# Two-stage packed attention and a mixer in one kernel: which engine copies the keys, when the first attention and w1's pieces are worked on, and in which iterations w2's pieces are made

## The chip, the core and the metric

The kernel runs on one core of a Trainium2 chip. A core has TensorE (PE in the profile, its weight loads PEld), VectorE (DVE), ScalarE (ACT), GpSimd (POOL) and SyncE (SP), which here issues all transfers. The metric is the device time of one execution in microseconds (us). Smaller is better.

## The reference

There are 8 batches of 8 heads, 576 tokens and 64 elements per head. A short sequence p of 32 tokens per head first attends to all keys; the 576 queries then attend to its 32 results. The output of all heads is x (576 by 512), and a mixer with float64 weights follows:

```python
p_packed = sm_attn(p, k, v)              # sm_attn: softmax(q k^T / 8) v
out = sm_attn(q, p_packed, p_packed)     # x = out, heads side by side: 8 x 576 x 512
h = x^T @ U @ V                          # over tokens, rank 32
u = x + h^T
ch = relu(u @ w_ch1) @ w_ch2             # 512 -> 2048 -> 512
return u + ch
```

w_ch1 (w1 below) and w_ch2 (w2) arrive as float64, and the kernel makes float32 of their bits itself.

## The kernel before, in words

**Two parts.** The *front* does the first attention stage for all batches (p against the keys) and makes float32 of w1. The *loop* does the mixer's two matrix products batch by batch, with the second attention stage of a later batch spread between them.

**The front** goes through 16 units, a batch's half of four heads each (`UN`, index i or u). For a unit it transposes the keys on TensorE (`a_turn`, which calls `turn` for h = 0, 1, 2), multiplies them with p (`a_scores`, line 244), takes the maximum on VectorE (line 448, tile mx) and the exponential on ScalarE (line 450), turns the result back (`a_turn_back`, lines 250, 252 and 459), multiplies with the values (`a_pack`, line 478) and turns the heads (`a_heads`, line 488). In `turn`, h = 0 and h = 1 each leave one PSUM bank that two copies of 128x256 empty into SBUF: one on ScalarE (line 231) and, while `split_copies` is True, one on VectorE (line 229). Queries (tile xT) go through the same `turn`.

Beside this the front makes w1's 16 pieces of 128x512 (`some_w1`): ScalarE takes the absolute value (line 143) and VectorE does four operations (lines 78 to 81) into w1t; the load four pieces ahead is issued there as well. `turns[i]` says how many pieces unit i gets. From unit 4 on each unit also takes three of the 24 steps of the second attention stage of batch 0 (`first = attention(0, res)`): query loads, turns, scores, softmax (with two GpSimd operations of 128x576, lines 283 and 294), `tokens` (lines 312, 313), `mix1` and `mix2` (line 333 and, on GpSimd, line 335, which writes al). al and ah are what the loop's first product reads. Steps and `a_p`, `a_heads` and `fold` share the two banks of the pool psT (t_ps). `fold(0, 0)` (lines 372, 378, 379) makes the first part of the folded w1 in unit 13. In the front the framework's planner arranges the instructions on each engine (the context is opened with `schedule_with_timeline_sim=True`), so their order is near the written one but not the same.

**The loop** starts behind `tc.manual_schedule()`: from there each engine works in the written order. For each batch b and each kt of 16, `gemm1(kt)` fills the banks h_ps (lines 86 to 88), ScalarE makes hh by a relu (line 614), VectorE hl (line 617); each half of h_ps has one bank only, so `gemm1(kt+1)` waits until hl(kt) has been made. `gemm2(kt-1)` then adds hh and hl times w2 into four banks o. At kt = 2, 6, 10 and 14 a `fold` follows, and steps of the attention of batch b + 1 (b + 2 in the later batches) are taken before, within and after `gemm2`.

**w2** is made during batch 0, a piece of 128 rows per iteration: `load_w2` (line 151, SP), `convert_w2` (line 77 on ScalarE, lines 78 to 81 on VectorE) and `split_w2` (line 158 on ScalarE, line 159 on VectorE), which leaves the high and the low part that `gemm2` reads. The pool for the bits has two buffers, that for the converted values four. At iteration kt the kernel splits piece kt + 1, loads kt + 3 and converts kt + 2. The place is after the fold and before the iteration's last step:

```python
if w2x:
    split_w2(*w2x)
    w2x = None
    if kt + 3 < NK:
        load_w2(kt + 3)
    if kt + 2 < NK:
        w2x = convert_w2(kt + 2)
```

The steps of batch 1's attention fall into batch 0's iterations as follows: softmax1(0) after w2 in kt = 4, softmax3(0) within gemm2 of kt = 6, softmax4(0) and the second scores in kt = 7, softmax1(1) at the head of kt = 8, softmax3(1) at the end of kt = 9, softmax4(1) in kt = 10, tokens from the end of kt = 11.

Of the kernel before, what the change touches and what calls it, by code (L numbers as in the profile page):

```python
# [19 lines left out]
def packed_attention_mixer_kernel(  # L20
# [37 lines left out]
    NK = DF // P  # L58
# [12 lines left out]
    def float32_of(x, t, raw, out=None, tested=False):  # L71


        low, high = raw[:, :, 0], raw[:, :, 1]
        out = x if out is None else out.bitcast(I32)
        if not tested:
            nc.scalar.activation(t, high.bitcast(F32), AF.Abs)
        nc.vector.tensor_single_scalar(t, t, LEAST, op=ALU.max)  # L78
        nc.vector.tensor_scalar(x, t.bitcast(I32), 3, 0x3FFFFFF8, op0=ALU.logical_shift_left, op1=ALU.bitwise_and)
        nc.vector.scalar_tensor_tensor(x, high, -0x40000000, x, op0=ALU.bitwise_and, op1=ALU.bitwise_or)  # L80
        nc.vector.scalar_tensor_tensor(out, low, 29, x, op0=ALU.logical_shift_right, op1=ALU.bitwise_or)
        return out.bitcast(F32)
# [12 lines left out]
    def bank():  # L95
        return psT.tile([P, 512], F32, name="t_ps", tag="t")
# [25 lines left out]
    def w2_parts(kt):  # L122
        return tuple(t[:, kt % 4] for t in w2t[kt // 4])

    def conv_tile(dtype):
        return pipe.tile([P, DM], dtype, name="os", bufs=4)

    def bits_tile():
        return pipe.tile([P, 512, 2], I32, name="bits", bufs=2)
# [19 lines left out]
    def load_w2(kt):  # L149
        b = bits["w2", kt] = bits_tile()  # L150
        nc.sync.dma_start(out=b.rearrange("p x t -> p (x t)"), in_=w2[kt * P:(kt + 1) * P, :])

    def convert_w2(kt):
        return kt, float32_of(conv_tile(I32), conv_tile(F32), bits.pop(("w2", kt)))

    def split_w2(kt, x):
        hi, lo = w2_parts(kt)
        nc.scalar.copy(hi, x)
        (nc.gpsimd if kt == 0 else nc.vector).tensor_tensor(lo, x, hi.bitcast(F32), op=ALU.subtract)
# [52 lines left out]
            out=x.rearrange("p (h y) -> p h y", h=2),  # L212
            in_=src[b, 4 * g:4 * g + 4].rearrange("(h z) (i c) d -> (z i) h (c d)", z=2, c=NT))

    split_copies = True

    def turn(t, x, h, bank):

        x = x.rearrange("p (h y) -> p h y", h=2)
        t_ps = bank()  # L220
        if h < 2:
            for j in range(4):
                o = P * (2 * (j % 2) + j // 2)
                nc.tensor.transpose(t_ps[:, o:o + P], x[:, h, P * j:P * j + P], ident)  # L224
            src = t_ps.rearrange("p (k a z i) -> p a z k i", k=2, a=2, z=2)
            for a in range(2):
                dst = t[:, 2 * h:2 * h + 2, :4 * I].rearrange("p z (k i a) -> p a z k i", k=2, a=2)[:, a]
                if a and split_copies:
                    nc.vector.tensor_copy(dst, src[:, a])
                else:  # L230
                    nc.scalar.copy(dst, src[:, a])  # L231
        else:
            for h in range(2):
                nc.tensor.transpose(t_ps[:64, P * h:P * h + P], x[:, h, SM:], ident)
            nc.scalar.copy(t[:64, :, LAST], t_ps[:64, :2 * P].rearrange("p (h i) -> p h i", h=4))
# [156 lines left out]
    ua = {}  # L392
    pn, pT, pps, sums = {}, {}, {}, {}

    def bank_a(tag):
        return lambda: psA.tile([P, 512], F32, name=f"{tag}_ps", tag=tag)
# [20 lines left out]
    def a_p(b):  # L417
        t_ps = bank()
        pT[b] = sA.tile([P, 2, P], F32, name="pT")
        pd = sA.tile([P, 2, 2, D], F32, name="pd", bufs=1)  # L420
        nc.gpsimd.tensor_copy(pd, pn[b].unsqueeze(2).to_broadcast([P, 2, 2, D]))
        for i in range(2):
            nc.tensor.transpose(t_ps[:, P * i:P * i + P], pd[:, i].rearrange("p z d -> p (z d)"), ident)
        nc.scalar.activation(pT[b][:, 0], t_ps[:, :P], AF.Copy, scale=scale)
        dst, src = (a.rearrange("p (y z n) -> p z y n", y=2, z=2) for a in (pT[b][:, 1], t_ps[:, P:2 * P]))
        for z in range(2):
            nc.scalar.activation(dst[:, z], src[:, 1 - z], AF.Copy, scale=scale)

    def a_turn(u):
        b, g = UN[u]  # L430
        if g == 0:
            a_p(b)
        ua[u]["t"] = sA.tile([P, 4, 5 * I], F32, name="kT")
        for h in range(3):
            turn(ua[u]["t"], ua[u]["x"], h, bank_a("k"))

    def a_scores(u):
        b, g = UN[u]
        s_ps = psA.tile([P, 1024], F32, name="s_ps", tag="s", bufs=1)
        scores(pT[b], ua[u]["t"], g, (s_ps[:, 512 - 5 * I:512], s_ps[:, 512:512 + 4 * I]))  # L440
        ua[u]["s"] = s_ps[:, 512 - 5 * I:512 + 4 * I]
# [10 lines left out]
    def a_turn_back(u, bank):  # L452
        b, g = UN[u]
        e1 = ua[u]["e"]
        eT = ua[u]["eT"] = sT.tile([P, 5, P], F32, name="eT")
        t_ps = bank()
        for kk in range(4):
            turn_back(t_ps, e1, kk, P * kk)
        nc.scalar.copy(eT[:, :4].rearrange("p k x -> p (k x)"), t_ps)
        t_ps = bank()  # L460
        turn_back(t_ps, e1, 4, 0)
        nc.scalar.copy(eT[:64, 4], t_ps[:64, :P])
        if g == 1 or b == B - 1:
            s = sums[b] if b < B - 1 else sums[b][:, g:g + 1]
            nc.gpsimd.tensor_scalar_add(s, s, 1e-9)
            nc.vector.reciprocal(s, s)
# [43 lines left out]
            load_w1(n + 4)  # L510


    turns = [0, 0, 1, 1, 1, 1, 2, 1, 1, 1, 2, 1, 1, 1, 1, 1]
    n_w1 = 0
    for i in range(NU):
        if i > 0:
            a_turn_back(i - 1, bank_a("m"))
        a_scores(i)
        if i + 1 < NU:
            a_load_v(i + 1)  # L520
            a_turn(i + 1)
        if i + 2 < NU:
            a_load(i + 2)
        a_softmax(i)
        if i < 2:
            load_w1(2 + i)
        for _ in range(turns[i]):
            some_w1(n_w1)
            n_w1 += 1
        if i > 1:  # L530
            a_pack(i - 2, bank_a("m"))
        if i > 2:
            a_heads(i - 3)
        if i >= 4:
            for _ in range(3):
                if first:
                    first.pop(0)()
        if i == 2:
            uv = load_uv()
        if i == 3:  # L540
            prepare_uv(*uv)
        if i == 13:
            fold(0, 0)
        if i == 14:
            load_w2(0)
            load_w2(1)
            steps = attention(1, res)
            steps.pop(0)()
            split_w2(*convert_w2(0))
            load_w2(2)  # L550
# [5 lines left out]
        lambda: (a_heads(NU - 1), tctx.close()),  # L556
    ]
    actx.close()
    split_copies = False


    ctx.enter_context(tc.manual_schedule())
# [118 lines left out]
            nc.sync.dma_start(out=out[b - 1 + i].rearrange("(i c) m -> c i m", c=NT)[8], in_=os_[I * i:I * i + I])  # L681

    w2x = convert_w2(1)

    for n in (20, 19, 18, 15, 15, 14, 13, 12, 12, 11, 5, 0, 0, 0, 0):
        steps.insert(n, lambda: None)
    last, parts = None, []
    for b in range(B):
        cur = Batch(b)
        oj = None  # L690
        ahead = attention(b + 2, res) if b + 2 < B else []
        for kt in range(NK):
            cur.gemm1(kt)
            if oj and kt == 1:
                store_joint(b - 1, oj)
            if steps and (b < 2 or kt % 4 != 2) and (b, kt) != (1, 0):
                steps.pop(0)()
            if (b, kt) == (0, 5):
                w2_tiles(ctx.enter_context(tc.tile_pool(name="sC", bufs=1, side="right", reuse_waits="tile")), 2)
            if kt > 0:  # L700
                cur.gemm2(kt - 1, (rest or steps).pop(0) if b == 0 and (rest or steps) else None)
            elif last:
                last.gemm2(NK - 1)
                last.store()
                if last.b % 2 == 1:
                    oj = joint(last.b, parts)
            if kt % 4 == 2 and (b, kt) != (B - 1, NK - 2):
                n = b * NPC + kt // 4 + 1
                fold(n // NPC, n % NPC)
            if w2x:  # L710
                split_w2(*w2x)
                w2x = None
                if kt + 3 < NK:
                    load_w2(kt + 3)
                if kt + 2 < NK:
                    w2x = convert_w2(kt + 2)
            if steps and kt % 4 != 2 and (b, kt) != (1, 0):
                steps.pop(0)()
            if kt == 1:
                cur.blocks()  # L720
            if kt == 3:
                cur.add_u()
            if ahead and kt == (13 if b else NK - 1):
                ahead.pop(0)()
            if kt == NK - 1 and b % 2 == 1:
                parts = [joint_parts(b, 0), joint_parts(b, 1)]
        assert not steps
        steps = ahead
        last = cur
# [35 lines left out]
```

## Time and profile before

| what | value |
|---|---|
| time, median of 3 runs (lowest to highest) | 846.15 us (845.97 to 846.75) |
| the profiled execution: its own time, its span | 845.35 us, 843.6 us |
| busy: PE, DVE, ACT, POOL | 813.0, 381.5, 328.0, 89.2 us |
| share of the span | 96%, 45%, 39%, 11% |
| read from HBM, written | 46.83 MB, 10.35 MB |

The span goes from the first to the last instruction; the execution's own time has the start and the end around it. Busy shares are means over the whole span, and the front and the loop have different limits, so the rows further down are by stretch. The busy time of PE is modelled at its ends. A wait names what released the waiting instruction last. [...]

### The profile page before, as it was taken

The page shows a single profiled execution, that of the slowest core. Times are in us where ns is not written, and L with a number is a line of the kernel's source. Part 1 is how long each engine was busy: PE and PEld are TensorE (multiplying, and loading weights), DVE is VectorE, ACT ScalarE, POOL GpSimd, SP SyncE. Part 2 cuts the span into 40 slices and gives each one's busy share as a digit, 9 for nine tenths or more (in the row PEclk, how much of TensorE's full clock was granted, in tenths as well). Part 3 has the DMA queues.
Part 4 walks back from the last instruction along what each step waited for, and adds up shares of the span by engine and source line. Part 5 has one row for each costly group of instructions (what it writes and reads, how often), then busy time and mean ns, then how long its engine had stood idle before and what let it go on. Part 6 is the DMA issues. An engine that isn't in the chain of part 4 may idle for free.

```text
span 843.6 us, 14585 instructions
## 1 busy us (share of the span) xinstructions
PE 813.0 (96%) x5800; PEld 653.9 (78%) x5800; DVE 381.5 (45%) x902; ACT 328.0 (39%) x1017; POOL 89.2 (11%) x131
## 2 busy tenths in 40 slices
PE   6888899999999999999999999999999999999997
PEld 4546478778878887888888888888788887888786
DVE  4899676984343333434333234333434234342231
ACT  4667764445233332334233332343234232332231
POOL 1322311100111001010011001010101011100000
PEclk9999999999999999999999999999999999999999
DMA  9999732331001100021001100110001100010001
GB/s 301 347 340 341 237 101 88 101 113 51 1 1 63 51 13 1 1 63 51 1 1 63 50 14 1 44 59 13 1 16 61 51 1 1 1 51 1 1 1 63
DMA packets 36245, 58.13 MB, mean 69 GB/s; under 512 B 9040, under 2 KB 19280, under 8 KB 36176
## 3 DMA queue, kind: packets, MB, share of 16 engines
q1 hardware_dynamic: 36176, 57.19, 20.6%
q8 instruction: 46, 0.75, 0.4%
q14 instruction: 23, 0.19, 0.1%
HBM read 46.83 MB, written 10.35 MB: 68 GB/s over the span
## 4 chain that ended last, share of the span: by engine, by line
PE 86%; DVE 7%; DMA 3%; ACT 2%; issue 1%; SPq 0%; ACTq 0%; DVEq 0%
PE o L86 17%; PE o L88 17%; PE o L87 16%; PE h_ps L86 9%; PE h_ps L88 8%; PE h_ps L87 8%; PE t_ps L372 4%; PE t_ps L224 1%; DMA bits<-in_moe_w_ch_dram 1%; PE t_ps L244 1%; DVE os L80 1%; PE t_ps L320 1%; DVE os L78 1%; DMA x<-in_moe_U_dram 1%; PE t_ps L250 1%
## 5 line engine op out<-in xcount | busy, mean ns | idle before, releaser
L86 PE MATMUL o<-w2h,hh 128*128 128x512 f32 x512 | 206.8, 404 | 0.0
L88 PE MATMUL o<-w2h,hl 128*128 128x512 f32 x512 | 202.5, 396 | 0.0
L87 PE MATMUL o<-w2l,hh 128*128 128x512 f32 x512 | 202.1, 395 | 0.0
L617 DVE SCALAR_TENSOR_TENSOR hl<-h_ps,hh 128x256 fp32r<-128x256 f32 x256 | 104.1, 422 | 201.0 <-ACT hj L616 188.8
L614 ACT ACTIVATE hh<-h_ps 128x256 fp32r<-128x256 f32 x256 | 98.7, 387 | 182.4 <-PE h_ps L88 181.8
L86 PE MATMUL h_ps<-ah,wth 128*128 128x320 f32 (+1 forms) x512 | 157.6, 308 | 2.1 <-DVE hl L617 2.0
L87 PE MATMUL h_ps<-al,wth 128*128 128x320 f32 (+1 forms) x512 | 151.6, 296 | 0.0
L88 PE MATMUL h_ps<-ah,wtl 128*128 128x320 f32 (+1 forms) x512 | 151.4, 296 | 0.0
L86 PEld LDWEIGHTS h_ps<-ah,wth 128*128 128x128 f32 x512 | 96.8, 189 | 34.8 <-issue 27.7
L88 PEld LDWEIGHTS o<-w2h,hl 128*128 128x128 f32 x512 | 96.5, 188 | 22.9
L86 PEld LDWEIGHTS o<-w2h,hh 128*128 128x128 f32 x512 | 96.8, 189 | 21.4 <-issue 4.6
L87 PEld LDWEIGHTS o<-w2l,hh 128*128 128x128 f32 x512 | 96.8, 189 | 16.8
L87 PEld LDWEIGHTS h_ps<-al,wth 128*128 128x128 f32 x512 | 96.9, 189 | 1.8
L88 PEld LDWEIGHTS h_ps<-ah,wtl 128*128 128x128 f32 x512 | 97.0, 189 | 0.0
L379 DVE TENSOR_TENSOR wtl<-t_ps,wth 128x256 fp32r<-128x256 f32 x128 | 48.5, 419 | 96.9 <-ACT wth L378 93.5
L378 ACT CAST wth<-t_ps 128x256 fp32r<-128x256 f32 x128 | 43.3, 374 | 109.2 <-PE t_ps L372 101.4
L335 POOL TENSOR_TENSOR al<-aT,ah 128x320 fp32r<-128x320 f32 (+1 forms) x32 | 25.7, 807 | 207.3 <-ACT ah L334 207.3
L283 POOL TENSOR_TENSOR e<-e,m 128x576 f32<-128x576 f32 x16 | 19.4, 1212 | 251.9 <-DVE m L282 251.9
L231 ACT COPY xT<-t_ps 128x256 f32<-128x256 f32 x60 | 20.3, 393 | 39.2 <-PE t_ps L224 38.5
L372 PE MATMUL t_ps<-w1t,ppT 64*32 64x512 f32 x512 | 35.0, 601 | 0.0
L334 ACT CAST ah<-aT 128x320 fp32r<-128x320 f32 (+1 forms) x32 | 13.7, 433 | 44.1 <-DVE aT L333 44.0
L294 POOL TENSOR_TENSOR e<-e,s 128x576 f32<-128x576 f32 x16 | 18.7, 1166 | 110.3 <-DVE s L293 110.2
(134 smaller groups left out, 964.7 us busy)
## 6 DMA issues: line engine op xcount, KB each, us to landing
bits<-in_moe_w_ch_dram SPq DMA_DIRECT2D x32, 512.0 KB, 5.2
kx<-in_k_dram SPq DMA_DIRECT2D x16, 576.0 KB, 7.1
x<-in_q_dram SPq DMA_DIRECT2D x16, 576.0 KB, 4.9
vt<-in_v_dram SPq DMA_DIRECT2D x32, 256.0 KB, 6.9
out_dram<-bits SPq DMA_DIRECT2D x32, 256.0 KB, 2.4
vt<-in_v_dram SPq DMA_DIRECT2D x16, 64.0 KB, 6.7
out_dram<-os SPq DMA_DIRECT2D x8, 128.0 KB, 2.3
ppTd<-ppTa SPq DMA_DIRECT2D x7, 128.0 KB, 3.7
```

What stands on the lines that cost most here:

```text
L86: nc.tensor.matmul(ps, lhsT=lh, rhs=rh, start=start, stop=False)
L87: nc.tensor.matmul(ps, lhsT=lh, rhs=rl, start=False, stop=False)
L88: nc.tensor.matmul(ps, lhsT=ll, rhs=rh, start=False, stop=stop)
L231: nc.scalar.copy(dst, src[:, a])
L283: nc.gpsimd.tensor_tensor(e, e, m.unsqueeze(2).to_broadcast([P, S // 32, 32]), op=ALU.subtract)
L294: nc.gpsimd.tensor_tensor(e, e, s.unsqueeze(2).to_broadcast([P, S // 32, 32]), op=ALU.mult)
L335: nc.gpsimd.tensor_tensor(al[:, g, ns], aT[:, ns], ah[:, g, ns].bitcast(F32), op=ALU.subtract)
L372: nc.tensor.matmul(f_ps[g][xs], lhsT=ppT[b][zs, g, xs], rhs=w1t[h // 2][zs, QW * c:QW * c + QW], start=True, stop=True)
L378: nc.scalar.copy(hi[:, g], f_ps[g][:, cs])
L379: nc.vector.tensor_tensor(lo[:, g], f_ps[g][:, cs], hi[:, g].bitcast(F32), op=ALU.subtract)
L614: nc.scalar.activation(hh[:, ms], src, AF.Relu)
L617: nc.vector.scalar_tensor_tensor(hl[:, ms], src, 0.0, hh[:, ms].bitcast(F32), op0=ALU.max, op1=ALU.subtract)
```

## The change

Three things change. First, `split_copies` goes; `turn` has an argument `split` that is False unless it is given, and `a_turn` gives True for h = 1 only. So in the front the second copy of h = 0, and the second copies of batch 0's queries, go to ScalarE. In the loop the copies were all on ScalarE already. Second, `turns` moves the second piece of units 6 and 10 to units 12 and 14, and the first attention starts at unit 6 in place of 4. Third, w2's pieces follow a list: iterations kt = 3 and kt = 6 of batch 0 make two pieces, kt = 8 and kt = 11 none, and each load is issued an iteration earlier (piece 3 ahead of the loop). Splits then run one piece further ahead after kt = 3, two after kt = 6, one after kt = 8, and as before from kt = 11 on.

```diff
--- before.py
+++ after.py
@@ -212,9 +212,7 @@
             out=x.rearrange("p (h y) -> p h y", h=2),
             in_=src[b, 4 * g:4 * g + 4].rearrange("(h z) (i c) d -> (z i) h (c d)", z=2, c=NT))
 
-    split_copies = True
-
-    def turn(t, x, h, bank):
+    def turn(t, x, h, bank, split=False):
 
         x = x.rearrange("p (h y) -> p h y", h=2)
         t_ps = bank()
@@ -225,7 +223,7 @@
             src = t_ps.rearrange("p (k a z i) -> p a z k i", k=2, a=2, z=2)
             for a in range(2):
                 dst = t[:, 2 * h:2 * h + 2, :4 * I].rearrange("p z (k i a) -> p a z k i", k=2, a=2)[:, a]
-                if a and split_copies:
+                if a and split:
                     nc.vector.tensor_copy(dst, src[:, a])
                 else:
                     nc.scalar.copy(dst, src[:, a])
@@ -432,7 +430,7 @@
             a_p(b)
         ua[u]["t"] = sA.tile([P, 4, 5 * I], F32, name="kT")
         for h in range(3):
-            turn(ua[u]["t"], ua[u]["x"], h, bank_a("k"))
+            turn(ua[u]["t"], ua[u]["x"], h, bank_a("k"), split=h == 1)
 
     def a_scores(u):
         b, g = UN[u]
@@ -510,7 +508,7 @@
             load_w1(n + 4)
 
 
-    turns = [0, 0, 1, 1, 1, 1, 2, 1, 1, 1, 2, 1, 1, 1, 1, 1]
+    turns = [0, 0] + [1] * 10 + [2, 1, 2, 1]
     n_w1 = 0
     for i in range(NU):
         if i > 0:
@@ -531,7 +529,7 @@
             a_pack(i - 2, bank_a("m"))
         if i > 2:
             a_heads(i - 3)
-        if i >= 4:
+        if i >= 6:
             for _ in range(3):
                 if first:
                     first.pop(0)()
@@ -556,7 +554,6 @@
         lambda: (a_heads(NU - 1), tctx.close()),
     ]
     actx.close()
-    split_copies = False
 
 
     ctx.enter_context(tc.manual_schedule())
@@ -681,6 +678,10 @@
             nc.sync.dma_start(out=out[b - 1 + i].rearrange("(i c) m -> c i m", c=NT)[8], in_=os_[I * i:I * i + I])
 
     w2x = convert_w2(1)
+    load_w2(3)
+
+    pieces = [1, 1, 1, 2, 1, 1, 2, 1, 0, 1, 1, 0, 1, 1, 1, 1]
+    n_w2 = 2
 
     for n in (20, 19, 18, 15, 15, 14, 13, 12, 12, 11, 5, 0, 0, 0, 0):
         steps.insert(n, lambda: None)
@@ -707,13 +708,15 @@
             if kt % 4 == 2 and (b, kt) != (B - 1, NK - 2):
                 n = b * NPC + kt // 4 + 1
                 fold(n // NPC, n % NPC)
-            if w2x:
-                split_w2(*w2x)
+            for _ in range(pieces[kt] if b == 0 else 0):
+                if w2x:
+                    split_w2(*w2x)
                 w2x = None
-                if kt + 3 < NK:
-                    load_w2(kt + 3)
-                if kt + 2 < NK:
-                    w2x = convert_w2(kt + 2)
+                if n_w2 < NK:
+                    w2x = convert_w2(n_w2)
+                    n_w2 += 1
+                    if n_w2 + 1 < NK:
+                        load_w2(n_w2 + 1)
             if steps and kt % 4 != 2 and (b, kt) != (1, 0):
                 steps.pop(0)()
             if kt == 1:
```

## Rows read from the trace of the kernel before

**Rows 1.** Stretches: us, busy PE PEld DVE ACT POOL, clock, DMA share, GB/s

```profile
26.00:60.00 34.00, 27.50 (x409) 18.30 (x412) 31.88 (x74) 23.31 (x74) 11.33 (x16) 0.90 1.05 337
...
60.00:82.00 22.00, 18.75 (x316) 12.42 (x301) 20.79 (x44) 16.41 (x46) 5.92 (x10) 0.92 1.04 342
...
82.00:104.50 22.50, 18.48 (x308) 11.43 (x306) 15.24 (x36) 15.78 (x51) 6.19 (x12) 1.00 0.81 256
...
104.50:843.60 739.10, 730.54 (x4625) 600.65 (x4620) 302.67 (x728) 258.73 (x811) 63.27 (x82) 1.00 0.10 34
```

**Rows 2.** The chain that ended last, 26 to 82 us, share by line

```profile
by line: DVE os L80 12.0%; DVE os L78 8.9%; DVE mx L448 8.6%; DVE w1t L81 8.4%; issue 7.7%; DMA bits<-in_moe_w_ch_dram 7.0%; DVE os L79 5.5%; DVE kT L229 5.4%; PE k_ps L224 4.0%; PE m_ps L250 3.4%; ACT os L143 3.1%; DVE vs L207 2.6%; PE s_p
```

**Rows 3.** Waits of TensorE, 104.5 to 190 us: total, times, longest us

```profile
PE h_ps L86 <- DVE hl L617: 2.0, 4, 0.8
```

**Rows 4.** Line 229, 26 to 82 us: min/median/max ns

```profile
L229 DVE COPY kT<-k_ps x18: 408/415/425, 26.9 to 77.8; 128x256 f32<-128x256 f32 x18
L229 DVE COPY xT<-t_ps x4: 405/408/421, 42.6 to 56.3; 128x256 f32<-128x256 f32 x4
```

**Rows 5.** Timeline of VectorE: start us, us, operation, count, idle before

```profile
57.01 0.41 DVE L229 COPY kT<-k_ps 128x256 f32<-128x256 f32 x1
...
57.35 0.76 DVE L298 STREAM_TRANSPOSE aT<-e 128x576 f32<-128x576 f32 x1
```

**Rows 6.** Groups of ScalarE, 26 to 104.5 us

```profile
L231 ACT COPY kT<-k_ps 128x256 f32<-128x256 f32 x23 | 8.5, 401 | 3.2 <-PE k_ps L224 2.8 <-PE s_ps L244 0.3
```

**Rows 7.** DMA issues, 105 to 195 us: count, KB each, us to landing

```profile
bits<-in_moe_w_ch_dram SPq DMA_DIRECT2D x13, 512.0 KB, 3.4
```

**Rows 8.** Timeline of VectorE in batch 0

```profile
129.77 0.96 DVE L617 SCALAR_TENSOR_TENSOR hl<-h_ps,hh 128x256 fp32r<-128x256 f32 x2 [2.17 <-ACT hj L616]
...
133.11 0.69 DVE L159 TENSOR_TENSOR w2l<-os,w2h 128x512 fp32r<-128x512 f32 x1 [1.62 <-ACT w2h L158]
...
144.93 1.62 DVE L379 TENSOR_TENSOR wtl<-t_ps,wth 128x256 fp32r<-128x256 f32 x4 [1.77 <-ACT wth L378]
...
146.64 0.69 DVE L159 TENSOR_TENSOR w2l<-os,w2h 128x512 fp32r<-128x512 f32 x1
...
149.51 0.75 DVE L617 SCALAR_TENSOR_TENSOR hl<-h_ps,hh 128x256 fp32r<-128x256 f32 x2
...
156.56 1.39 DVE L78 TENSOR_SCALAR os<-os 128x512 f32<-128x512 f32 x1
```

**Rows 9.** Timeline of ScalarE in batch 0

```profile
149.62 0.62 ACT L158 CAST w2h<-os 128x512 fp32r<-128x512 f32 x1 [1.78 <-DVE os L81]
```

**Rows 10.** Timeline of TensorE in batch 0, first products of three iterations

```profile
149.98 0.41 PE L86 MATMUL h_ps<-ah,wth 128*128 128x320 f32 x1
...
160.25 0.41 PE L86 MATMUL h_ps<-ah,wth 128*128 128x320 f32 x1 [0.48 <-DVE hl L617]
...
171.71 0.42 PE L86 MATMUL h_ps<-ah,wth 128*128 128x320 f32 x1 [0.76 <-DVE hl L617]
```

**Rows 11.** Timeline of GpSimd in batch 0

```profile
156.19 1.47 POOL L283 TENSOR_TENSOR e<-e,m 128x576 f32<-128x576 f32 x1 [11.74 <-DVE m L282]
```

**Rows 12.** Line 78, whole front and batch 0: min/median/max ns

```profile
L78 DVE TENSOR_SCALAR os<-os x34: 243/422/1387, 11.7 to 181.8; 128x512 f32<-128x512 f32 x32, 128x160 f32<-128x160 f32 x1, 128x144 f32<-128x144 f32 x1
```

**Rows 13.** Timelines of VectorE, TensorE and GpSimd at the front's end

```profile
78.71 0.75 DVE L448 TENSOR_REDUCE mx<-s_ps 128x1 f32<-128x576 f32 x1
...
80.71 0.33 PE L488 MATMUL t_ps<-ident,two 128*128 128x128 f32 x1 [1.83 <-DVE x L313]
...
89.12 0.76 DVE L448 TENSOR_REDUCE mx<-s_ps 128x1 f32<-128x576 f32 x1 [1.81 <-PE s_ps L244]
...
91.18 2.25 POOL L335 TENSOR_TENSOR al<-aT,ah 128x320 fp32r<-128x320 f32 x3 [1.96 <-ACT ah L334]
...
100.24 0.75 DVE L448 TENSOR_REDUCE mx<-s_ps 128x1 f32<-128x576 f32 x1
...
104.49 0.42 PE L86 MATMUL h_ps<-ah,wth 128*128 128x320 f32 x1
```

## The prediction

> **What bounds the kernel now.** I read the busy times by stretch first [rows 1]. They show two regimes. From 104.5 us on TensorE is busy 730.54 of 739.10 us: there only what makes TensorE wait counts. Before that (the front: keys, first attention, w1) TensorE works with gaps, VectorE is busy 31.88 of 34 us and 20.79 of 22 us, the transfers run at a share of 1.05 and 1.04, and only from 82 us on do both let go (15.24 of 22.5 us and 0.81). So two things can set the front's pace, and the chain of waits chooses between them: from 26 to 82 us it names mostly VectorE lines, the largest L80, L78, L448 and L81, with one transfer of w1 at 7.0% [rows 2]. From 82 us no engine is near full and transfers are not either [rows 1]: short waits in queues that work in order.
>
> In the loop the view of waits names one stall of TensorE that matters: h_ps waits for hl, four times, 2.0 us in all up to 190 us [rows 3]. All of it lies in batch 0, where VectorE still makes w2.
>
> **The change part by part.**
>
> *Copies from VectorE to ScalarE.* Of a unit's two VectorE copies (L229) the one of h = 0 goes to ScalarE, and so do all four of the first attention's queries. From 26 to 82 us VectorE does 18 of the keys' and the 4 of the queries' [rows 4]; 9 + 4 = 13 of them leave. Where VectorE runs without a gap, a copy of 0.41 us moves the next start by 0.34 us (57.01 to 57.35) [rows 5]. So 13 x 0.34 = 4.4 us of VectorE time leave the stretch where it is busy 52.67 of 56 us. Copies after 82 us I cost at nothing: VectorE is idle 7.3 us there. ScalarE gets 20 copies of 0.40 us [rows 6] in the whole front, at most 8 us on 55.5 us busy of 78.5 [rows 1]: still below VectorE's 67.9 us there, so that is covered unless ScalarE's order delays an exponential.
>
> *First attention two units later, w1's doubles two and four units later.* No work is removed. Attention's 24 steps run in units 6 to 13 in place of 4 to 11; the q loads go behind two more units' loads on SP. The second w1 piece of units 6 and 10 moves to 12 and 14, with the loads four pieces ahead. Each piece is L78, L79, L80, L81, some 2.2 us of VectorE (a w2 piece's 2.87 us less its L159 of 0.69 [rows 8]), two pieces 4.4 us, out of the full stretch into the tail, where 7.3 us are idle. If all of that fits into idle places, the front gains 4.4 us more; if it lies on the tail's chain, nothing. I take nothing: the tail's idle places are waits within in-order queues, and attention's last steps go there too.
>
> Front: 4.4 us earlier; bounds 8.8 us earlier (4.4 + 4.4) and 1.5 us later (below).
>
> *w2.* Each piece has ScalarE's L158, VectorE's L159, ScalarE's L77 of the next piece and VectorE's L78 to L81. Iterations kt = 3 and 6 now do two, 8 and 11 none; each piece's bits are asked for an iteration earlier. Transfers: a landing takes 3.4 us there [rows 7], two iterations 10.27 us (first products at 149.98 and 160.25 [rows 10]), and each load has about one iteration: hidden. If one were late, ScalarE's L77 would stop and the relu (L614) behind it, and with that hl.
>
> kt = 3 has room: hl there came after 2.17 us of VectorE idle, and the next piece after another 1.62 us [rows 8]. The second piece costs 2.87 us (L159 at 146.64 to hl at 149.51) [rows 8] plus 0.73 us, because its L158 can start only when L81 has ended and takes 0.62 us (149.62 to 150.24, against 149.51) [rows 9]. 3.6 us go into 3.8 us of idle: nothing, bound 0.3 us.
>
> kt = 6 has none. The fold's L379 ends at 146.5, w2 runs to 149.51, then hl, and TensorE's next first product (gemm1 of kt = 8) starts at 149.98, right behind it [rows 8, 10]. A second piece puts hl at 149.51 + 3.6 = 153.1, also because kt = 7's relu is then queued on ScalarE behind the second L158, which waits for VectorE. TensorE then starts at 153.6: 3.6 us lost at once. It comes back where VectorE catches up: kt = 8 has no piece, so the wait of 0.48 us at 160.25 goes, and that of 0.76 us at 171.71 [rows 10]. kt = 7 stays as full as before, so nothing is gained there. Fold and softmax steps between follow TensorE's and GpSimd's times, so an empty slot in kt = 8 partly becomes idle time: 3.6 - 0.48 - 0.76 = 2.4 us later. Bounds: 0 (all caught up) and 3.9 us (nothing, and kt = 3's 0.3).
>
> At kt = 8 L78 took 1.39 us, where the median of its kind is 0.42, beside GpSimd's subtraction of 1.47 us [rows 8, 11, 12]: an empty kt = 8 saves 0.97 us of VectorE. The Trainium skill (SBUF — State Buffer, "SBUF: two separate sides") says that GpSimd and a two-port VectorE operation hold a shared port pair exclusively, for a whole instruction. The row agrees: L78 ends 0.29 us after GpSimd's. If the whole 0.97 us reached TensorE, the loop's loss would be 1.4 us; without it 2.4 us. I keep 2.4, since TensorE waited only 0.48 us there.
>
> **Sum.** Profiled execution 845.35 us (span 843.6): -4.4 + 2.4 = -2.0, so 843.35. It lies 0.8 us below the median of 846.15, so 844.15 us is predicted, 0.24% faster. What this kernel's measurement can tell from no change I take as 0.2%, 1.7 us.
>
> **The rivals.**
>
> *Transfers set the front* (slower). Share 1.05 and 1.04 until 82 us [rows 1], and the bytes that must come before the last unit are the same in number. Then a faster VectorE waits for them, the front gains nothing, and the loop's 2.4 us remain: 848.55. It decides if unit 11's mx comes no earlier than 78.71 us [rows 13]. Against it: the chain names transfers for 7.0% only [rows 2], and after unit 11 the next mx comes 10.4 us later, at 89.12 [rows 13], where the transfers no longer press.
>
> *First attention ends too late* (same). Its last al now ends at 93.43 us, gemm1 starts at 104.49: 11.06 us to spare. Two units (mx of 12 to mx of 14, 89.12 to 100.24) are 11.12 us [rows 13]. So the spare time is just used up, and every us more is a us of the front. The attention's tokens also hold the two t banks: L488 waited 1.83 us for them [rows 13]; this now meets fold(0, 0) and unit 14. At 3 us: 847.15; wholly on top of an unchanged front, it is the 1.5 us later named above.
>
> *The double at kt = 6 is caught up.* Loop 0: 841.75. It needs VectorE to be idle nowhere from kt = 8 to 11; against it stand the fold and GpSimd's multiplication, which arrive by their own clocks.
>
> *The tail takes w1 for nothing.* Front 8.8 us: 839.75. For it: 7.3 us idle [rows 1]; against it: the 10.4 us between two mx [rows 13] are a chain of attention's mix, not of w1.
>
> **How the numbers follow.** Forecast 0.43 (its own range 842.5 to 846), transfers 0.18, late attention 0.17, caught up 0.12, tail free 0.10. Faster: 0.24 of the forecast's share, all of the last two, 0.46. Same: 0.16 of the forecast, 0.13 of the late attention, 0.02 of the transfers, 0.31. Slower: the rest, 0.23. The range goes from the free tail (839.75) to the transfers' rival: 839.7 to 848.6; what lies beyond, front -8.8 with loop 0 and the later front, I give 2 in 10.
>
> **What would show it.** Front: L229 20 times fewer; VectorE below 94% in 26 to 82 us; gemm1's first product near 100 us; unit 11's mx well before 78.71. Loop: a wait of some 3.6 us of h_ps for hl near kt = 8, none at kt = 10 and 12, and the stretch from the first product to the end 2.4 us longer than 739.1. Wrong if the first product stays at 104.5, if it waits for GpSimd's al, or if no long wait stands at kt = 8.

## The result, and the profile after

The changed kernel takes 851.53 us (median of 7, 848.43 to 852.24) against 846.60 us for the kernel before, run beside it: a ratio of 1.0047 (95% interval 1.0032 to 1.0062), 4.0 us slower. Here and below the ratio is taken over all executions and is not that of the two medians, which lie 4.9 us apart here. Forecast were 844.15 us and a range up to 848.6 us. Its profiled execution, read here, took 851.63 us (span 849.9, mean granted clock 0.985); that of before took 845.35 us (span 843.6, clock 0.991). Of the changed kernel's seven executions the two with a mean granted clock of 0.994 and 0.995 took 848.43 and 849.57 us, the five with 0.985 to 0.990 took 851.09 to 852.24. Lines have moved: VectorE's copy of the keys is L227, ScalarE's L229, mx L446, the fold L370 to L377, the heads L486, the attention's last mix L330 to L333, hl L614.

By stretch, to be read beside [rows 1] (from and to, us, then each engine's busy time, the granted clock, the transfers' share and GB/s):

```profile
26.00:60.00 34.00, 30.17 (x493) 20.24 (x494) 29.21 (x66) 28.17 (x93) 5.96 (x14) 0.95 1.06 349
60.00:82.00 22.00, 16.37 (x279) 11.73 (x277) 19.41 (x38) 16.44 (x51) 7.37 (x12) 0.92 1.07 349
82.00:104.50 22.50, 18.30 (x266) 11.00 (x266) 17.90 (x34) 15.21 (x48) 8.84 (x15) 1.00 0.71 226
104.50:849.90 745.40, 733.35 (x4622) 604.09 (x4622) 302.18 (x730) 259.37 (x814) 61.69 (x80) 0.99 0.10 34
```

VectorE did lose its work: 29.21 and 19.41 us instead of 31.88 and 20.79, 87% of the 56 us. The transfers are as full as before. The same stretch's chain of waits, grouped by line:

```profile
by line: DMA bits<-in_moe_w_ch_dram 25.6%; DMA vt<-in_v_dram 12.0%; DMA ppTd<-ppTa 11.9%; PE k_ps L222 9.2%; DVE os L80 5.2%; DVE mx L446 3.7%; PE s_ps L242 3.7%; PE m_ps L248 3.6%; PE m_ps L476 3.4%; DVE w1t L81 2.1%; PE t_ps L197 2.1%; is
```

In [rows 2] VectorE's lines led and a transfer had 7.0%; now three transfers hold 49.5%. Yet the front did not simply stand still. Timelines of VectorE, TensorE and GpSimd over its second half, beside [rows 13]:

```profile
60.91 0.75 DVE L446 TENSOR_REDUCE mx<-s_ps 128x1 f32<-128x576 f32 x1
72.70 0.75 DVE L446 TENSOR_REDUCE mx<-s_ps 128x1 f32<-128x576 f32 x1
...
98.79 0.38 PE L330 MATMUL t_ps<-vs,ms 128*128 128x256 f32 x1 [0.84 <-DVE aT L331]
99.12 1.06 PE L370 MATMUL t_ps<-w1t,ppT 64*32 64x512 f32 x8
...
100.59 2.87 POOL L333 TENSOR_TENSOR al<-aT,ah 128x320 fp32r<-128x320 f32 x3 [1.07 <-ACT ah L332]
100.65 1.09 DVE L79 TENSOR_SCALAR os<-os 128x512 int32<-128x512 int32 x1
101.77 1.10 DVE L80 SCALAR_TENSOR_TENSOR os<-bits,os 128x512 int32<-128x512 int32 x1
...
103.13 0.88 DVE L81 SCALAR_TENSOR_TENSOR os<-bits,os 128x512 int32<-128x512 int32 x1
103.93 0.74 DVE L446 TENSOR_REDUCE mx<-s_ps 128x1 f32<-128x576 f32 x1
...
105.06 0.33 PE L486 MATMUL t_ps<-ident,two 128*128 128x128 f32 x1 [1.80 <-DVE wtl L377]
...
106.17 0.39 PE L86 MATMUL h_ps<-ah,wth 128*128 128x320 f32 x1
```

Unit 9's mx is at 60.91 us; before it was at 68.36, 7.5 us earlier. Unit 10's is at 72.70 against 73.39: 11.8 us for one unit. Experiments 4, 7 and 10, with the later attention, show such a step of 9 to 12 us at this place; the kernel before has its long step two units earlier, from unit 7 to unit 8 (52.94 to 62.31). So the 7.5 us are for the most part a step that the kernel before has behind it by then, and not a gain. The last unit's is at 103.93 against 104.12. Then gemm1's first product needs 2.24 us more, against 0.37 before (104.12 to 104.49): TensorE stands for 1.80 us before the heads' product until the fold's wtl is made. The fold's products (99.12) stand right behind the attention's last mix (98.79). Before, the two were far apart (TensorE's timeline of the kernel before, two rows not shown yet):

```profile
90.33 0.38 PE L332 MATMUL t_ps<-vs,ms 128*128 128x256 f32 x1 [0.84 <-DVE aT L333]
...
96.05 1.22 PE L372 MATMUL t_ps<-w1t,ppT 64*32 64x512 f32 x16
```

The chain that ended last, from 94 us to the first product, shows what else is on this path (two rows of it):

```profile
94.33 5.12 DMA bits<-in_moe_w_ch_dram
...
104.77 0.68 ACT e L448
```

It is the load of w2's piece 1, issued when w1's last piece has left its buffer (its L81 ends at 94.31), then that piece's conversion (L77 to L81), and behind it in the queues the last unit's mx and exponential, the fold's last wth and the heads' product. Three of the conversion's operations run beside GpSimd's al and take 1.09, 1.10 and 0.88 us; in the kernel with the copies alone, whose al is done at 87.23 us, the same three take 0.42, 0.68 and 0.69: 1.28 us less.

So the loop starts 1.68 us later in this execution, not 4.4 earlier. The rest is lost in the loop. The waits of TensorE from 106 to 196 us (line, what it waited for, us in all, times, longest), beside [rows 3]:

```profile
PE h_ps L86 <- DVE hl L614: 4.1, 2, 3.6
PE t_ps L486 <- ACT ppTa L487: 0.7, 1, 0.7
PE t_ps L486 <- DVE e L274: 0.4, 1, 0.4
```

VectorE in iteration kt = 6, from the end of the fold to hl, beside [rows 8]:

```profile
148.24 1.62 DVE L377 TENSOR_TENSOR wtl<-t_ps,wth 128x256 fp32r<-128x256 f32 x4 [1.81 <-ACT wth L376]
149.96 0.69 DVE L159 TENSOR_TENSOR w2l<-os,w2h 128x512 fp32r<-128x512 f32 x1
...
153.59 0.69 DVE L159 TENSOR_TENSOR w2l<-os,w2h 128x512 fp32r<-128x512 f32 x1 [0.69 <-ACT w2h L158]
...
156.44 0.75 DVE L614 SCALAR_TENSOR_TENSOR hl<-h_ps,hh 128x256 fp32r<-128x256 f32 x2
```

From the first L159 to hl it is 6.48 us; with one piece it was 2.87 us. The second piece adds 3.61 us, of which 0.69 us is VectorE waiting for ScalarE's L158. TensorE pays all of it at gemm1(8), and something more behind it:

```profile
156.91 0.41 PE L86 MATMUL h_ps<-ah,wth 128*128 128x320 f32 x1 [3.64 <-DVE hl L614]
...
158.76 0.63 PE L86 MATMUL o<-w2h,hh 128*128 128x512 f32 x1
...
162.01 0.40 PE L88 MATMUL o<-w2h,hl 128*128 128x512 f32 x1
...
162.93 0.31 PE L86 MATMUL h_ps<-ah,wth 128*128 128x320 f32 x1
```

Two us after the wait a product of 512 columns takes 0.63 us, where it took 0.40 before; at 162 us it is 0.40 again. The granted clock in stretches of this kernel (columns as in the first fence) says why:

```profile
107.00:111.00 4.00, 4.00 (x20) 3.92 (x20) 2.31 (x5) 2.46 (x7) 0.00 (x0) 0.57 0.10 33
150.00:156.90 6.90, 3.27 (x27) 1.70 (x25) 6.01 (x12) 2.68 (x7) 0.00 (x0) 1.00 0.24 76
156.90:163.00 6.10, 6.09 (x25) 5.20 (x26) 5.87 (x12) 1.74 (x5) 0.00 (x0) 0.72 0.30 96
```

Behind a stretch with TensorE busy 3.27 of 6.90 us, the clock is 0.72 on the mean, that is about half of the stretch at the level of 1.2 GHz. gemm1(8) to gemm1(9) took 6.02 us, against 5.13 us before; in experiments 2 and 3, which have no such wait, it is 5.13 us too.

The difference adds up from the starts of gemm1(kt) in the two traces, after less before: 1.68 us at kt = 0, 2.67 at kt = 2, 3.28 at kt = 5, 6.93 at kt = 8, 7.82 at kt = 9, 6.29 at kt = 16 and from there on the same. The spans differ by 6.3 us. The 1.0 us between kt = 0 and 2 goes with a stretch at a low clock (0.57 from 107 to 111 us), which some executions have and some do not (last section). The 0.61 us from kt = 2 to kt = 5 are read in experiment 2.

### The profile page after: what moved, and what is told of

Read it like the earlier page. It is cut to its first block, busy times and chain, and to the rows that moved or that the text cites. A ratio compares the mean times of both kernels' runs of the same rounds, so it can differ in the third digit from the quotient of the medians.

```text
span 849.9 us, 14604 instructions
## 1 busy us (share of the span) xinstructions
PE 815.7 (96%) x5800; PEld 657.7 (77%) x5800; DVE 377.5 (44%) x882; ACT 331.2 (39%) x1037; POOL 86.1 (10%) x131
## 4 chain that ended last, share of the span: by engine, by line
PE 87%; DMA 6%; DVE 3%; ACT 2%; issue 2%; SPq 0%; POOL 0%; ACTq 0%; POOLq 0%
PE o L86 17%; PE o L88 17%; PE o L87 17%; PE h_ps L86 9%; PE h_ps L87 8%; PE h_ps L88 8%; PE t_ps L370 4%; DMA bits<-in_moe_w_ch_dram 3%; DMA vt<-in_v_dram 1%; PE t_ps L222 1%; PE t_ps L242 1%; PE t_ps L318 1%; DVE os L80 1%; PE t_ps L248 1%; PE k_ps L222 1%
## 5 line engine op out<-in xcount | busy, mean ns | idle before, releaser
L614 DVE SCALAR_TENSOR_TENSOR hl<-h_ps,hh 128x256 fp32r<-128x256 f32 x256 | 104.2, 422 | 202.8 <-ACT hj L613 189.9
L377 DVE TENSOR_TENSOR wtl<-t_ps,wth 128x256 fp32r<-128x256 f32 x128 | 48.5, 419 | 97.1 <-ACT wth L376 93.8
L333 POOL TENSOR_TENSOR al<-aT,ah 128x320 fp32r<-128x320 f32 (+1 forms) x32 | 26.3, 826 | 207.3 <-ACT ah L332 207.3
L281 POOL TENSOR_TENSOR e<-e,m 128x576 f32<-128x576 f32 x16 | 18.6, 1162 | 260.7 <-DVE m L280 260.7
L229 ACT COPY xT<-t_ps 128x256 f32<-128x256 f32 x64 | 21.4, 395 | 39.2 <-PE t_ps L222 38.5
L370 PE MATMUL t_ps<-w1t,ppT 64*32 64x512 f32 x512 | 36.0, 601 | 0.0
```

What stands on the lines that cost most here:

```text
L281: nc.gpsimd.tensor_tensor(e, e, m.unsqueeze(2).to_broadcast([P, S // 32, 32]), op=ALU.subtract)
L333: nc.gpsimd.tensor_tensor(al[:, g, ns], aT[:, ns], ah[:, g, ns].bitcast(F32), op=ALU.subtract)
L370: nc.tensor.matmul(f_ps[g][xs], lhsT=ppT[b][zs, g, xs], rhs=w1t[h // 2][zs, QW * c:QW * c + QW], start=True, stop=True)
L377: nc.vector.tensor_tensor(lo[:, g], f_ps[g][:, cs], hi[:, g].bitcast(F32), op=ALU.subtract)
L614: nc.vector.scalar_tensor_tensor(hl[:, ms], src, 0.0, hh[:, ms].bitcast(F32), op0=ALU.max, op1=ALU.subtract)
```

## The experiments

Each kernel is the kernel before with the edit named; of edits that the diff above already has, only the lines that tell them apart are shown, or none. All compute the whole reference. Medians are given with that of the kernel before on the same chip, then the ratio with its 95% interval.

**1. w2's part alone.**

```diff
+    load_w2(3)
+    pieces = [1, 1, 1, 2, 1, 1, 2, 1, 0, 1, 1, 0, 1, 1, 1, 1]
...
+            for _ in range(pieces[kt] if b == 0 else 0):
```

> Only w2's list of pieces; the front is that of the kernel before. If the double at kt = 6 is what costs time in the loop: first product of the loop at 104.5 us as before, one wait of h_ps for hl of some 3.6 us before gemm1 of kt = 8, a lower granted clock right after it, and 3 to 4 us (0.4%) slower in all. If the loss comes from the front alone: within 1 us of before.

850.62 us against 846.33: 1.0050 (1.0034 to 1.0067). This part alone makes the whole loss. TensorE's timeline and clock after the wait in this kernel:

```profile
155.04 0.63 PE L86 MATMUL h_ps<-ah,wth 128*128 128x320 f32 x1 [3.64 <-DVE hl L617]
```
```profile
155.00:158.20 3.20, 3.16 (x13) 3.17 (x14) 3.06 (x7) 1.39 (x4) 0.00 (x0) 0.53 0.50 164
```

The same 3.64 us, and again a stretch near the lower level behind it (0.53). From gemm1(4) to gemm1(16) it takes 68.87 us, before 65.63: 3.24 us lost.

**2. One double, and none at kt = 6.**

```diff
-    pieces = [1, 1, 1, 2, 1, 1, 2, 1, 0, 1, 1, 0, 1, 1, 1, 1]
+    pieces = [1, 1, 1, 2, 1, 1, 1, 1, 0, 1, 1, 1, 1, 1, 1, 1]
```

> The front of before; w2 with the double at kt = 3 only, none at kt = 8, one everywhere else. If the double at kt = 6 is the whole loss of the loop: no wait over 1 us at kt = 8, the wait at kt = 10 (0.48 us) gone, and with kt = 3 costing at most 0.6 us the time is within 0.7 us of before. If working ahead as such costs (kt = 3's double, the loads): 1.5 us or more slower.

845.93 against 846.09: 0.9996 (0.9984 to 1.0009). Two of TensorE's waits:

```profile
PE h_ps L86 <- DVE hl L617: 1.3, 3, 0.5
PE t_ps L488 <- DVE e L276: 0.2, 1, 0.2
```

The long wait is gone, and the loss with it; gemm1(4) to gemm1(16) takes 65.07 us, before 65.63. The double at kt = 3 is not free: gemm1(4) to gemm1(5) takes 5.82 us, before 5.38. It is not hl(4) that TensorE stands for there: hl(4) ends at 132.07 and gemm1(5) starts at 134.10. The second row says what it is: the heads' product (L488) waits until VectorE's softmax has read a bank t_ps (L276), and L276 stands behind the second piece and hl in VectorE's queue (131.99 us; 130.65 in the kernel before). L488 starts 0.38 us later than before, counted from gemm1(4). In the changed kernel this is the row of 0.4 us in the view of waits above. The empty kt = 8 gives that back, and no more can be told from the median.

**3. The second double one iteration earlier,** at kt = 5, where VectorE has some idle time:

```diff
-    pieces = [1, 1, 1, 2, 1, 1, 2, 1, 0, 1, 1, 0, 1, 1, 1, 1]
+    pieces = [1, 1, 1, 2, 1, 2, 1, 1, 0, 1, 1, 0, 1, 1, 1, 1]
```

> The front of before; w2 as in the change, but its second double at kt = 5 in place of 6. If a double costs what VectorE has no idle time for before the next hl: some 0.8 us at kt = 7 and 1 to 2 us at kt = 8, 1 to 2.5 us slower in all (0.1 to 0.3%). If any double in the softmax's neighbourhood costs its full 3.6 us: as slow as the double at kt = 6, 0.5%.

847.15 against 846.09: 1.0017 (0.9999 to 1.0035), not clear of no change. In its profiled execution, which took 850.11 us, gemm1(6) to gemm1(7) takes 6.93 us, before 5.77, at a granted clock of 1.00. In the loop no wait of h_ps for hl is above 0.53 us; the loss lies inside the fold's group of products (timelines of TensorE, its weight loads, ScalarE and VectorE):

```profile
147.89 2.24 PE L372 MATMUL t_ps<-w1t,ppT 64*32 64x512 f32 x16
```
```profile
149.07 0.15 PEld L372 LDWEIGHTS t_ps<-w1t,ppT 64*32 64x32 f32 x8 [1.03 <-ACT xT L235]
```
```profile
145.81 0.62 ACT L158 CAST w2h<-os 128x512 fp32r<-128x512 f32 x1 [2.43 <-DVE os L81]
```
```profile
149.33 0.75 DVE L617 SCALAR_TENSOR_TENSOR hl<-h_ps,hh 128x256 fp32r<-128x256 f32 x2
```

The group takes 2.24 us (1.09 before). Its second half waits 1.03 us for a bank t_ps that ScalarE's copies of the queries empty (L235, 148.66 to 149.02). These copies stand in ScalarE's queue behind the second piece's L158, which has waited 2.43 us for VectorE. hl ends at the same moment as the group (149.33 + 0.75 = 150.08; gemm1(7) starts at 150.07), so whether hl alone would have held gemm1(7) as long is open. A second piece thus costs what TensorE next needs from any queue that the piece delays, and how much later that comes: a bank that VectorE reads at kt = 3 (0.44 us), a bank that ScalarE empties at kt = 5 (about 1.2 us), hl at kt = 6 (3.64 us).

**4. The whole front's part** (copies, w1's later doubles, later attention), w2 as before.

> All three edits of the front, w2's old schedule in the loop. If front and loop add up: first product near 106 us (1.7 us later than before), no wait over 1 us near kt = 8, and 1 to 3 us slower than before (0.1 to 0.3%). If the loop's loss hung on the changed front: as slow as the whole change, 4 us or more.

846.57 against 846.33: 1.0006 (0.9994 to 1.0018). The front's three edits together bring nothing. Its end, in TensorE's timeline:

```profile
96.08 0.38 PE L330 MATMUL t_ps<-vs,ms 128*128 128x256 f32 x1 [0.84 <-DVE aT L331]
96.42 1.06 PE L370 MATMUL t_ps<-w1t,ppT 64*32 64x512 f32 x8
...
102.60 0.33 PE L486 MATMUL t_ps<-ident,two 128*128 128x128 f32 x1 [2.05 <-DVE wtl L377]
...
103.71 0.39 PE L86 MATMUL h_ps<-ah,wth 128*128 128x320 f32 x1
```

The pattern is that of the changed kernel, 2.5 us earlier: mix, fold right behind it, a wait for wtl, the first product. The wait for wtl by itself is no sign of the later attention: with the copies alone there is one too (experiment 5). What sets the kernels with the later attention apart is the end: from the start of the last unit's mx to the first product they take 2.0 to 4.2 us (the changed kernel, experiments 4, 7 and 10), all others 1.1 us or less.

**5. The copies alone.**

```diff
-            turn(ua[u]["t"], ua[u]["x"], h, bank_a("k"))
+            turn(ua[u]["t"], ua[u]["x"], h, bank_a("k"), split=h == 1)
```

> Only the copies moved from VectorE to ScalarE. If VectorE sets the pace of the front: first product 1 to 4.4 us earlier (100 to 103.5 us), the time 0.1 to 0.5% lower. If transfers set it: first product within 1 us of 104.5, no change of time. If ScalarE's queue in its order becomes the limit: later than 105.5 us.

844.51 against 846.33: 0.9980 (0.9966 to 0.9994). Faster by 1.7 us, 4.4 were forecast. Unit 11's mx comes at 72.43 us, 6.3 us earlier than in [rows 13], but the first product at 102.54, only 2.0 earlier. The chain of 26 to 82 us, and what is waited for in the tail (timelines of ScalarE and TensorE):

```profile
by line: DMA bits<-in_moe_w_ch_dram 14.7%; DMA vt<-in_v_dram 8.7%; issue 6.7%; DVE os L80 6.0%; PE k_ps L222 5.8%; DVE w1t L81 4.8%; PE s_ps L242 4.7%; ACT kT L229 4.4%; DVE os L79 4.2%; DVE mx L446 3.8%; DVE os L78 3.7%; PE m_ps L476 3.4%;
```
```profile
98.57 0.67 ACT L77 ACTIVATE os<-bits 128x512 f32<-128x512 f32 x1 [2.43 <-DMA bits<-in_moe_w_ch_dram]
```
```profile
100.17 0.45 PE L486 MATMUL t_ps<-ident,two 128*128 128x128 f32 x1 [2.78 <-DVE wtl L377]
```

With VectorE relieved, two transfers are the chain's largest lines already by this edit (23.4% together; VectorE's lines, as far as shown, add up to 22.5%). In the tail ScalarE waits 2.43 us for bits of w2, whose load was issued only at 93.00 us. The fold's casts to wth stand behind that L77 in ScalarE's queue, and the heads' product of TensorE then waits 2.78 us for wtl.

**6. Copies and w1's later doubles.**

```diff
+    turns = [0, 0] + [1] * 10 + [2, 1, 2, 1]
```

> Copies and w1's later doubles, the attention where it was, w2 as before. The copies alone gave 0.2%, all three edits of the front nothing, the later attention alone nothing. If w1's later doubles take the gain (the last conversion later, so w2's load of piece 1 later): no faster than before within 0.1%. If the attention takes it only together with the copies: as fast as the copies alone, 0.2% faster than before.

844.59 against 846.68: 0.9971 (0.9958 to 0.9985). Not told apart from the copies alone within the intervals. So what spends the copies' gain in experiment 4 is the later attention: 3.0 us from here (0.9971 to 1.0006, on two chips), 2.2 us from experiment 5 (0.9980 to 1.0006, on one chip).

**7. Later attention alone.**

```diff
-        if i >= 4:
+        if i >= 6:
```

> Only the first attention two units later. If its mix and the fold meet the last units: first product 1 to 4 us later (105.5 to 108.5), slower by 0.1 to 0.5%. If the front is set by the bytes that must arrive, or by VectorE's total work: first product within 1 us of 104.5, no change.

846.66 against 846.33: 1.0004 (0.9993 to 1.0015). Timelines of TensorE, VectorE and GpSimd at its front's end:

```profile
100.48 0.39 PE L332 MATMUL t_ps<-vs,ms 128*128 128x256 f32 x1
...
100.66 0.76 DVE L448 TENSOR_REDUCE mx<-s_ps 128x1 f32<-128x576 f32 x1 [1.09 <-PE s_ps L244]
...
100.80 1.06 PE L372 MATMUL t_ps<-w1t,ppT 64*32 64x512 f32 x8
...
104.14 0.72 POOL L335 TENSOR_TENSOR al<-aT,ah 128x256 fp32r<-128x256 f32 x1
...
104.81 0.39 PE L86 MATMUL h_ps<-ah,wth 128*128 128x320 f32 x1
```

This shows the trade most plainly. The last unit's mx comes 3.5 us earlier than before (100.66 against 104.12), with VectorE's units 4 and 5 free of attention. But the attention's last mix is now at 100.48 in place of 90.33, the fold starts behind it, GpSimd's last al ends at 104.86, and the first product comes 0.3 us later than before. What the keys gain, attention and fold take.

**8. Copies, and batch 1's query load later** (issued at the loop's start, out of the way of the loads that the tail waits for).

```diff
-            steps.pop(0)()
+            load_q1 = steps.pop(0)
...
     ctx.enter_context(tc.manual_schedule())
+    load_q1()
```

> Copies only, and batch 1's queries are loaded at the loop's start in place of unit 14. If bytes in the last units hold up the front now that VectorE has less to do (the chain of the run with the copies only names q's load for 21.5% of its last 20 us): first product 1 to 3 us earlier than the 102.5 us there. If the front's end hangs on VectorE's or ScalarE's order: within 0.7 us of it.

844.84 against 846.09: 0.9978 (0.9963 to 0.9993), as the copies alone. Its profiled execution has the first product at 100.68 us, 1.9 us earlier than experiment 5's, which is what the first branch expected. But that execution took 842.74 us, 2.1 us less than the median, and unit 11's mx is 1.2 us earlier already (71.26 against 72.43), ahead of anything that the edit moves. The medians show no gain from the queries' bytes.

**9. Copies, and w1's last piece loaded into the other pool of buffers.** w2's second load uses the buffer that w1's last piece leaves, its first load that of w1's piece 13; by this edit they get those of pieces 11 and 13:

```diff
-        b = bits["w1", n] = bits_tile() if n % 2 else ...
+        b = bits["w1", n] = bits_tile() if n % 2 and n < 15 else ...
```

> Copies only, and w1's last piece is loaded into the other pool of bits, so that w2's load of piece 1 need not wait until that piece is converted. If this chain (w1's last conversion, w2's load, L77 in ScalarE's order, the last units behind it) sets the front's end: that load is issued near 85 us in place of 93, L77 waits less than 0.5 us in place of 2.43, first product 1 to 3 us earlier than 102.5. If not: within 0.7 us of it.

842.32 against 846.09: 0.9952 (0.9935 to 0.9969), 4.1 us faster (3.8 between the medians) and the best of all. SyncE's issue and ScalarE's use:

```profile
80.76 0.33 SPq L151 DMA_DIRECT2D bits<-in_moe_w_ch_dram  x1
```
```profile
93.03 0.71 ACT L77 ACTIVATE os<-bits 128x512 f32<-128x512 f32 x1
```

The second load goes out at 80.76 us instead of 93.00 (the first at 71.72 instead of 80.03), and ScalarE does not wait for bits. The first product, which was to come 1 to 3 us earlier than 102.5, is at 103.91 in this profiled execution; that execution took 2.4 us more than the median, with a low clock in the front (last section). Experiment 12, with the same front, has it at 101.74, 0.8 us earlier. So the gain is shown by the medians, and only in part by the traces.

**10. That buffer with the whole front, and 11. that buffer alone.**

> All three edits of the front, w2's old schedule, and w1's last piece loaded into the other pool of bits. If w1's later doubles cost only by holding back w2's load: as fast as the copies with that other buffer (0.48% faster than before), within 0.1%. If later attention and doubles cost VectorE time in the last units by themselves: 0.2 to 0.3% slower than that, so some 0.2% faster than before.

846.21 against 846.68: 0.9994 (0.9978 to 1.0010). With the late attention the buffer brings nothing that can be measured: no bits are waited for, but the fold's products start at 98.44 us right behind the last mix, as in experiment 4, and the first product is at 104.86 (103.71 there; here with a granted clock of 0.87 from 82 to 100 us).

> The kernel before, only w1's last piece in the other pool of bits; copies as before. If w2's late load binds only once VectorE has less to do: within 0.1% of before. If it bound the front before as well: 0.2 to 0.3% faster, and the copies add the rest to 0.48%.

848.34 against 846.68: 1.0026 (1.0003 to 1.0049). Neither branch came: alone it is slower. Here the front's order comes out differently. Unit 13's mx follows unit 12's after 7.9 us (88.54 to 96.44), before after 4.5 us, and TensorE stands long before the fold (TensorE's timeline):

```profile
97.30 1.22 PE L372 MATMUL t_ps<-w1t,ppT 64*32 64x512 f32 x16 [2.92 <-ACT pT L427]
```

So the gain of experiment 9 is not the buffer's wait alone, and 2.43 us may not be booked to it. One part can be seen: the pieces' conversion, moved up, now runs beside GpSimd's al (91.50 to 94.16), and VectorE's pairs of L79 and L80 take 1.86 and 1.82 us, before 0.75 and 1.29. Which of the moved steps makes the order good with the copies and bad without them was not found.

**12. Experiment 9, and no double, with kt = 8 empty** (w2's pieces one each, all one iteration later from kt = 8 on).

```diff
+    pieces = [1] * 8 + [0] + [1] * 7
```

> Copies, the other buffer for w1's last piece, and w2 with no piece at kt = 8 and no double (each piece from 8 on is made one iteration later, still before it is used). If the double at kt = 3 costs 0.4 us and the empty kt = 8 gains 1 us: 1 us better than the copies with that buffer, 0.55 to 0.65% faster than before, first products of kt = 4 to 16 about 64.6 us apart in place of 65.63. If the just-in-time pieces make gemm2 wait: slower than 0.48%.

843.71 against 846.68: 0.9956 (0.9938 to 0.9974), not better than experiment 9 (0.9952). The gain at kt = 8 came (gemm1(9) to gemm1(10) 4.49 us, before 5.14) and was given back at the end, where the pieces are made just in time: gemm1(15) to gemm1(16) takes 5.77 us, before 5.06, and gemm1(16) to gemm1(17) 5.60, before 4.39. TensorE's waits name w2's pieces (w2h 0.4 us, w2l 0.2 us twice) and, at 192.38 us, batch 1's al (0.4 us). That is the expectation's second branch.

## Why the prediction failed

**The front's sum was wrong.** The step that failed is "Front: 4.4 us earlier", made of two terms. The copies' 4.4 us gave 1.7 to 2.5 us (experiments 5 and 6): VectorE's copies left as counted (unit 11's mx comes 6.3 us earlier), but the tail waits for a load and a buffer, which the term did not look at since it ended at 82 us. And "First attention two units later ... I take nothing" was 2.2 to 3.0 us (experiments 5 and 6 to 4). Together 0.5 us later (1.0006), within measurement of nothing. The bound of 1.5 us later was not worked out (3 us on an unchanged front are 3 us), and the profiled execution's 1.68 us lie beyond it.

**The rival "first attention ends too late" was right,** with a price near its 3 us. It named two ways, al and the t banks that meet the fold. TensorE does not wait for al, which in the changed kernel has ended at 103.46. The fold does follow the last mix within 0.33 us (98.79 to 99.12), and the heads' product waits 1.80 us for wtl. But there is a third way that the prediction did not name: w2's conversion, which now runs beside al, takes 1.28 us longer than in experiment 5, and the chain that ended last goes through it. With w2's load moved up (experiment 10) the conversion is out of al's way, yet the first product comes no earlier, with the fold again right behind the mix. What each of these is worth no run separates. I weighed it at 0.17 with "the spare time is just used up"; a slack of 11.06 us against a delay of 11.12 us, with the fold's own 7 to 8 us behind the attention (98.79 to 106.17; 96.08 to 103.71), was no slack.

**The rival "transfers set the front" was half right.** Its test was unit 11's mx no earlier than 78.71 us. It came at 77.60 in the changed kernel, but at 72.43 with the copies alone, so transfers do not forbid the gain. They do become the chain's largest lines once VectorE is relieved (14.7% and 8.7%; 25.6% for one with all three edits), which [rows 2] could not show as long as VectorE led.

**w1's later doubles at nothing: right** (experiment 6 against 5).

**The loop's mechanism was right, its size off.** The wait at gemm1(8) was forecast at 3.6 us and is 3.64; hl waits for the whole second piece including L158; the waits behind it go or shrink: 1.53 us come back from kt = 9 to kt = 16 (7.82 to 6.29), 1.24 forecast. Forecast 2.4, measured 3.6 us in the changed kernel (2.67 at kt = 2 to 6.29) and 3.2 with w2's part alone. Two terms were too small. kt = 3's double, booked at 0 with a bound of 0.3, costs 0.61 us (2.67 to 3.28) and 0.44 in experiment 2. Of the 3.8 us of idle time that the prediction filled, 1.62 us lie behind hl(4); the second piece so pushes hl(4) and the softmax's transposes behind it, and TensorE waits for the bank that these read. And the stretch at a low clock behind the wait, 0.89 us (6.93 to 7.82), was not a term at all. "The double at kt = 6 is caught up" is refuted.

**The shared port.** With kt = 8 empty, GpSimd's subtraction took 1.16 us (L281 at 163.12) against 1.47 [rows 11], and line 78's slowest from 105 to 195 us is 0.42 us against 1.39 [rows 12]. The rows agree with the rule of the Trainium skill (SBUF — State Buffer, "SBUF: two separate sides") that the prediction used: with no VectorE piece beside it, GpSimd's operation is shorter too. In the loop it decided little: gemm1(9) to gemm1(10) became 0.75 us shorter (5.14 to 4.39), where the prediction counted on the wait of 0.48 us. At the front's end, where the prediction did not look for it, the conversion beside al lost more (1.28 us).

**Sum.** Front by experiment 4, 0.5 us (0.06%), and loop by experiment 1, 4.2 us (0.50%), make 4.7 us; the whole change measures 4.0 us (2.7 to 5.2 by its interval). Experiment 1's 4.2 us is more than its 3.24 us from kt = 4 to 16; in its profiled execution 0.83 us are lost from kt = 0 to 4 with a low clock. Experiments 4 and 5, with w2 as before, lose 1.0 and 0.8 us there too, so w2's list is not needed for that; the rest is open.

## What to carry to other kernels

Before you double a piece of work in an in-order queue, list what stands behind it there and in the queues that wait for it, and what of that the busy engine needs next: a result, or a bank that must come free. Read the idle time ahead of each; idle time behind it does not count. Where there is none, the piece was paid in full, and the busy engine ran slower for a while after it had waited. A chain that is moved later is free only up to its slack, and the slack ends at whatever stands behind the chain in shared banks and queues, here the fold, and at what runs beside it at its new place, here w2's conversion. When you relieve the engine that sets a stage's pace, ask in the same step which transfer and which buffer comes next.

## What the runs showed of the hardware

The same code runs with low-clock stretches in different places. The changed kernel and experiment 4 have the same front; from 30 to 36 us (stretch windows of the two):

```profile
30.00:36.00 6.00, 4.30 (x31) 3.07 (x31) 5.65 (x15) 4.86 (x15) 0.62 (x2) 0.72 1.09 330
```
```profile
30.00:36.00 6.00, 4.96 (x68) 3.44 (x71) 6.00 (x16) 4.65 (x17) 0.62 (x2) 1.00 1.08 340
```

At a granted clock of 0.72 against 1.00 unit 5's mx comes at 43.47 instead of 40.79 us. Of that lag of 2.7 us, 0.7 us were there at unit 2's mx (25.18 against 24.45), and 2.5 us are left at the first product (106.17 against 103.71). Experiments 6 and 9 show 0.72 there as well, and their profiled executions are 2.2 and 2.4 us above their own medians. At the loop's start the clock falls in some executions (0.57 here from 107 to 111 us; 0.53 in experiment 1 from 104 to 107 us) and stays 1.00 in others (before, experiments 9 and 12): gemm1(0) to gemm1(4) then takes 24.3 to 24.8 us instead of 23.6. What sets this off is open. A front of this kernel read from a single profile is therefore good to some 2 us only; the verdicts above rest on all executions of each kernel.
